# One load of the filter's rows for two blocks, in long runs, in a one-core gated mix of a state-space convolution and a spectral filter

## The chip, the cores and the metric

The kernel runs on one core of a Trainium2 chip. TensorE (PE) multiplies matrices into PSUM, VectorE (DVE), ScalarE (ACT) and GpSimd (POOL) work element by element, and SyncE (SP) issues every transfer of this kernel into one queue, in program order. The metric is the device time of one execution in microseconds (us), as the median of three runs. Lower is better.

## The reference

The input `u` has 2048 positions and 640 channels. Two results are made from it and mixed by a gate:

```python
g = _sigmoid((x * gate_w).sum(-1, keepdims=True))
# a: a long convolution of every channel with a generated kernel, plus a skip
P = jnp.exp((A * dt[:, None])[:, :, None] * pos[None, None, :])
K = 2.0 * jnp.einsum("dn,dnl->dl", C, P).real
y = jnp.fft.irfft(Uf * Kf[None, :, :], L2)[:, :, :L]
a = y + u * D_skip[None, None, :]
# b: a 2-D FFT filter over positions and channels
X = jnp.fft.rfft2(x, axes=(-2, -1)) * (w_r + 1j * w_i)
b = jnp.fft.irfft2(X, s=(S, D), axes=(-2, -1))
return g * a + (1 - g) * b
```

## The kernel before

All FFTs are products with small matrices of cosines and sines. The 640 channels are permuted and cut into four **blocks** of 160; blocks 0 and 1 are one **half**, blocks 2 and 3 the other. The work has these parts, in the order in which the code writes them down:

- `params`: the parameters of the generated kernel, in three bf16 parts each, written to DRAM (`pm_d`, `pp_d`).
- `columns`: the forward transform of `u` along the positions. `stage1` multiplies (L694) and transposes on DVE (L696), `stage2` multiplies (L711, L706), ACT copies the result out of PSUM (L756) and it is written to DRAM as `u_d` (L758).
- `responses`: the convolution kernels, from exponentials and sines on ACT (L973, L985), products on POOL and DVE (L994, L999, L1002) and matmuls (L972, L984, L1015); they go to DRAM as `k_d` (L1022).
- `gates`: the row sums for the gate.
- `spectral`: for nine groups of frequencies, the transform along the channels, the filter, and the way back (L801 to L904). `back2` multiplies (L904), ACT copies (L906), and the rows of the filtered result are written to `s3e_d`, a DRAM tensor of the form (half, 64 rows, 32 places, 320 columns), by L910 and L912. A row of 320 columns holds the 160 columns of one block and then the 160 of the other block of its half.
- `convolution`: for each block, `first` reads `k_d` (L1062) and does stage 1 of it (L694, L696). Nine calls of `unit` follow: stage 2 (L711; L706 for the odd ninth), the product with `u_d` on DVE (L1072, L1073) and POOL (L1074, L1075), and the matmuls of the way back (L1088, L1087), copied by ACT (L1090). The `u_d` that they need is read by L1145 and, for two units at a time, by L1149. Then `final` brings both results together.

`final(c, s3)` is the function in question. It first loads `te`, the filter's rows for block `c`: two transfers (L1099), one per 64 partitions, each 64 partitions x 16 places x 160 columns, that is 640 KB in runs of 640 bytes. They read what all 34 writes of that half to `s3e_d` have left, so they wait for these. Eight places of `te` at a time are multiplied by a small matrix (L1106) and scaled by the gate into `oe` on ACT (L1109). DVE transposes the convolution's result (L1113), PE multiplies it (L1121), ACT scales it into `ot` (L1126, L1127), POOL (DVE in block 3) adds `oe` (L1129), and L1131 writes the block to the output. `te`, `oe` and `ot` are one buffer each: the load for block `c` waits for the last matmul on the `te` of block `c - 1`.

The order of the instructions is not that of the code. Every operation is first noted as a unit with its inputs, outputs and a cost; a list scheduler (`order`) then picks, engine by engine, the ready unit of the highest rank. The rank is the length of the work behind the unit plus a number per function and engine, from the table `OPT["bias"]`. `OPT` also holds how far an engine looks ahead (`slack`), what a change of matmul shape on PE must gain (`hold`) and what a change of ACT's function table must (`table`). Where the scheduler foresees an idle PE, it puts in matmuls on a dead PSUM bank, which nothing reads (L265). So other numbers in `OPT` give another order of the whole program, SP's queue included, with the same work in it.

Of the kernel before, what the change touches and what calls it, by code (L numbers as in the profile page):

```python
# [151 lines left out]
    pass  # L152


OPT = {"bias": {"phases.DVE": -458537, "kgen.PE": -2536869, "unit.PE": -1194301, "mags.PE": -331203, "columns_head.SP": 260860, "columns.SP": -693714, "params.POOL": -110164, "back2.ACT": -2261149, "final.DVE": -992306, "filt.DVE": 1107470, "F": -1039852, "convolution.ACT": -592301, "front.SP": -1514751, "back2.PE": -1325765, "K": -7913, "first.SP": 1842522, "kgen.DVE": -1054315, "parts.DVE": 962846, "final.SP": 35999, "unit.ACT": 946495, "back1.POOL": 569005, "spectral.SP": -145917, "back1.DVE": 2832979, "front.DVE": -311958, "A": -375686, "params.ACT": 1555504, "front.POOL": 552518, "stage1.DVE": -353411, "convolution.SP": 251538, "unit.POOL": 1784148, "gates.DVE": -376347, "transposes.ACT": -1106844, "columns.ACT": -1333182, "back1.ACT": -83186, "parts.SP": -217602, "final.ACT": 263248, "parts.POOL": -507299, "turned.PE": -815648, "channels.ACT": -43187, "back2.SP": -726481, "params.SP": 1202525, "body.SP": -341452, "stage2.PE": 549111, "P": 705000, "final.PE": -711277, "mags.ACT": -1704667, "G": -861810, "final.POOL": 840381, "params.DVE": 151878, "kgen.ACT": -164284, "kgen.SP": -984011, "channels.DVE": 689109, "C": 828378, "stage1.PE": 535690, "product.PE": -44746, "gates.SP": -143744, "load.SP": 1167739, "phases.POOL": -21833, "unit.DVE": -288316, "transposes.PE": 469985, "turned.ACT": 852484, "turns.SP": -557358, "second_table.SP": 378902, "table.SP": 324454, "constants.SP": -319603}, "slack": {"SP": 830, "PE": 134, "POOL": 1971, "ACT": 222, "DVE": 38}, "hold": 47607, "table": 289533}


class Unit:
# [876 lines left out]
def convolution(T, A, out):  # L1035
    R, V, G, S, P, Y = T.R, T.V, T.G, T.S, T.P, T.Y
    z = Space(R, T.left)
# [56 lines left out]
    gate = lambda x, j, a: T.gate[:, x, 8 * j + a:8 * j + a + 1]  # L1094

    def final(c, s3):
        te, oe, ot = tep(), oep(), otp()
        for j in range(2):
            Y.dma_start(te[64 * j:64 * j + 64], T.s3e_d[c // 2, :, 16 * j:16 * j + 16, 160 * (c % 2):160 * (c % 2) + 160], reads=[("e", k, c // 2) for k in range(16)] + [("e1", c // 2)])  # L1099
# [15 lines left out]
        for k, (a, n) in enumerate(AS):  # L1115
            p = fin()[:, :, 0:160 * n].rearrange("p j (a d) -> p j a d", a=n)
# [20 lines left out]
    for c in range(4):  # L1137
        if c == 1:
            for pool, x in more:
                pool.bases = pool.bases + x.bases  # L1140
        side = [first(c + 1, t1[c + 1])] if c < 3 else []
        if c:
            side.append(final(c - 1, s3[c - 1]))
        ux = uxp()
        Y.dma_start(ux[:32].rearrange("p r d -> p (r d)"), T.u_d[c, :32, 16].rearrange("p r d -> p (r d)"), reads=[("u", c, 16)])  # L1145
        unit(c, t1[c], s3[c], 8, ux[:32].unsqueeze(1))
        for g in range(0, 8, 2):
            u = up()
            Y.dma_start(u, T.u_d[c, :, 0:16].rearrange("p (s g) r d -> p s g (r d)", s=2)[:, :, g:g + 2], reads=[("u", c, x) for x in (g, g + 1, g + 8, g + 9)])  # L1149
# [31 lines left out]
```

## Time and profile before

| | before |
|---|---|
| median of 3 runs | 568.64 us (567.94 to 571.13) |
| the profiled execution | 570.62 us |
| its span, first to last instruction | 568.8 us |
| mean granted clock of TensorE | 0.947 |
| PE busy | 456.8 us (80%) |
| DVE busy | 446.3 us (78%) |
| ACT busy | 327.7 us (58%) |
| POOL busy | 278.9 us (49%) |
| SP's transfers, packet time of 16 DMA engines | 47.3% |

The profiled execution took 1.8 us more than its span, and 2.0 us more than the median. All times below that stand without a unit at the left of a row are microseconds from the start of the span. In a timeline, a row gives the start, the time to the end of the last instruction in it, the engine, the line, the operation with its shape, the number of instructions (xN), and in brackets the idle time ahead of it with what ended it. An f32 matmul stands twice in the profile (x32) for each one in the program (x16). In the list of instructions of the order, xN counts the program's.

### The profile page before, as it was taken

What the parts mean: (1) busy time and instruction counts of PE and PEld (TensorE: products, weight loads), DVE (VectorE), ACT (ScalarE), POOL (GpSimd) and SP (SyncE); (2) the same over time, 40 slices, a digit from 0 to 9 for tenths busy, and PEclk for the clock granted to TensorE, in tenths of its full rate; (3) what the DMA queues carried; (4) which work ended last, traced back from release to release, by engine and by line L of the source; (5) the groups of instructions that cost most, each with busy time, mean ns of one, the idle gap of its engine ahead of it and who ended that gap; (6) DMA issues with size and microseconds to landing.
All of it is one profiled execution on the core that took longest, in us unless ns stands there. A gap on an engine that the chain in (4) does not pass through costs nothing. (4 is left out here: it accounts for less than half of the span.)

```text
span 568.8 us, 17984 instructions
## 1 busy us (share of the span) xinstructions
PE 456.8 (80%) x7712; PEld 263.6 (46%) x7712; DVE 446.3 (78%) x631; ACT 327.7 (58%) x593; POOL 278.9 (49%) x254
## 2 busy tenths in 40 slices
PE   0577769689788997998989889888988578879884
PEld 0133325345455655655555565645645234334351
DVE  7899349975499899887897978969996775787353
ACT  3131397598865986888787887222433153446553
POOL 0087006315685494674658556426243331847640
PEclk9988899899898999999999999979999897999897
DMA  8856775635711341423322234652354865384704
GB/s 260 338 187 193 264 245 178 196 122 207 237 52 52 103 136 29 140 51 106 103 78 77 57 96 116 197 156 87 94 141 148 186 115 149 119 202 120 187 2 185
DMA packets 50839, 81.22 MB, mean 143 GB/s; under 512 B 4324, under 2 KB 37288, under 8 KB 50760
## 3 DMA queue, kind: packets, MB, share of 16 engines
q1 hardware_dynamic: 50760, 80.08, 47.3%
q8 instruction: 60, 0.98, 0.7%
q14 instruction: 19, 0.16, 0.1%
HBM read 51.64 MB, written 28.43 MB: 141 GB/s over the span
## 5 line engine op out<-in xcount | busy, mean ns | idle before, releaser
L994 POOL TENSOR_TENSOR sb<-sb 128x512 f32<-128x512 f32 x80 | 111.6, 1423 | 98.7 <-ACT sb L985 89.3
L696 DVE STREAM_TRANSPOSE sb<-ps 128x1024 f32<-128x1024 f32 x40 | 80.1, 2020 | 23.3 <-PE ps L694 23.3
L984 PE MATMUL ps<-sb 52*128 52x512 bf16 x480 | 74.0, 387 | 14.4 <-DVE sb L1002 9.8
L694 PE MATMUL ps<-sb 64*128 64x512 f32 x160 | 55.1, 768 | 36.9 <-DMA sb<-in_u_l 18.3
L973 ACT ACTIVATE sb<-ps 128x512 f32<-128x512 f32 (+1 forms) x80 | 63.2, 824 | 13.1 <-PE ps L972 12.3
L1074 POOL TENSOR_TENSOR sb<-sb 128x320 f32<-128x320 f32 (+1 forms) x36 | 31.2, 866 | 77.0 <-DVE sb L1072 39.3
L711 PE MATMUL ps<-sb 64*32 64x160 f32 x2048 | 57.8, 323 | 7.5 <-DVE sb L1073 2.8
L985 ACT ACTIVATE sb<-ps 128x1024 f32<-128x1024 f32 x40 | 41.2, 1029 | 27.4 <-PE ps L984 26.7
L1090 ACT COPY sb<-ps 128x640 f32<-128x640 f32 (+1 forms) x40 | 30.0, 749 | 45.5 <-PE ps L1088 41.4
L1072 DVE TENSOR_TENSOR sb<-ps,sb 128x640 f32<-128x640 f32 (+1 forms) x36 | 28.0, 776 | 35.4 <-PE ps L711 13.0
L801 PE MATMUL ps<-sb 128*128 128x161 f32 (+4 forms) x280 | 49.5, 317 | 7.6 <-DVE sb L891 7.6
L1002 DVE TENSOR_TENSOR sb<-sb,ps 128x512 f32<-128x512 f32 x80 | 51.4, 678 | 0.0
L711 PEld LDWEIGHTS ps<-sb 64*32 64x32 f32 x2048 | 33.4, 109 | 36.8 <-issue 12.5
L756 ACT COPY sb<-ps 128x320 f32<-128x320 f32 (+1 forms) x68 | 25.6, 436 | 41.4 <-PE ps L711 25.5
L801 PEld LDWEIGHTS ps<-sb 128*128 128x128 f32 (+2 forms) x280 | 39.6, 187 | 18.7 <-issue 15.1
L999 DVE SCALAR_TENSOR_TENSOR sb<-sb,ps 128x512 f32<-128x512 f32 x40 | 27.3, 682 | 26.7 <-ACT ps L985 26.7
L985 ACT ACTIVATE ps<-ps 128x1024 f32<-128x1024 f32 x40 | 40.8, 1021 | 9.4 <-PE ps L984 6.5
L1088 PE MATMUL ps<-sb 32*64 32x160 f32 x1024 | 36.5, 326 | 12.0 <-issue 5.1
L984 PEld LDWEIGHTS <-sb 52*128 52x128 bf16 x480 | 24.2, 96 | 45.7 <-issue 34.4
L1015 PE MATMUL ps<-sb 128*32 128x64 f32 x2560 | 44.6, 222 | 0.0
L1015 PEld LDWEIGHTS ps<-sb 128*32 128x32 f32 x2560 | 38.4, 111 | 12.9 <-issue 10.1
L694 PEld LDWEIGHTS ps<-sb 64*128 64x128 f32 x160 | 15.8, 222 | 53.5 <-DVE sb L696 24.9
(128 smaller groups left out, 876.7 us busy)
## 6 DMA issues: line engine op xcount, KB each, us to landing
sb<-u_d SPq DMA_DIRECT2D x24, 640.0 KB
u_d<-sb SPq DMA_DIRECT2D x32, 320.0 KB
sb<-in_w_l SPq DMA_DIRECT2D x8, 642.0 KB
sb<-in_u_n SPq DMA_DIRECT2D x8, 640.0 KB
k_d<-sb SPq DMA_DIRECT2D x20, 256.0 KB
s3e_d<-sb SPq DMA_DIRECT2D x32, 160.0 KB
sb<-s3e_d SPq DMA_DIRECT2D x8, 640.0 KB
out<-sb SPq DMA_DIRECT2D x3, 1280.0 KB
```

The lines of the kernel that those rows point to most:

```text
L694: T.P.matmul(p[:, h].rearrange("p (d q a) -> p d q a", d=2, q=8), T.e1[l], x[l, :, i:i + 8], start=True, stop=True)
L696: T.V.transpose(t1[:, g:g + 8].rearrange("p g k d -> p g d k"), p.rearrange("p h (g d a) -> p (h g) d a", d=4, a=32))
L711: T.P.matmul(o[i][32 * j:32 * j + 32], T.w2[l, 4 * g + j, 32 * ri:32 * ri + 32], t1[l, :, 4 * g + j], start=True, stop=True)
L801: P.matmul(p[:, 161 * i:161 * i + n], lhs(i, part), tab(i)[part][0], start=i == 0, stop=False)
L973: u = S.activation(ef[:, :, c:c + n], p[:, :, :n], AF.Exp)
L984: P.matmul(p[:, h, :], st.pp[l, zz], turns[l, v, s], start=s == 0, stop=s == 2)
L985: u = S.activation(p if o is None else o, p if o is None else p.rearrange("p h (v c) -> p h v c", v=2), AF.Sin, scale=TWO_PI)
L994: G.tensor_tensor(out=y[:, v], in0=e[:, :, 64:96], in1=sc[:, 1 - v], op=ALU.mult)
L1002: V.tensor_tensor(out=xh[:, 0, h].rearrange("p d (y j) -> p d y j", y=2), in0=eh[:, h, :, 0:64].rearrange("p d (y j) -> p d y j", y=2), in ...
L1015: P.matmul(st.pb[32 * r:32 * r + 32, o, :], y[:, ri, 4 * qq + r, :], x[:, ri, 4 * qq + r, :], start=t % 2 + qq + 1 - ri == 0, stop=t % 2 + ...
L1074: G.tensor_tensor(out=t2[:nl, 0, :n], in0=ma[:nl, :n, 0], in1=ma[:nl, :n, 1], op=ALU.subtract)
L1088: P.matmul(q[o, j - js[0], 0:160], w3[l, 2 * g + s, ri, :], t2[l, ri, s, :], start=ri == 0, stop=ri == 1)
```

## The change

`te` becomes a tile of 16 places x 320 columns: the rows for both blocks of a half. It is loaded when `c` is even, by two transfers of 64 partitions x 5120 numbers (1280 KB each). In DRAM the 16 places of a row lie one behind the other, so every partition's part is one run of 20 KB. Blocks 0 and 1, and then blocks 2 and 3, take their 160 columns out of the same tile, so there are four transfers instead of eight, with the same bytes. The matmuls read the tile with a step of 320 instead of 160 from place to place. `oe` and `ot` lie 2560 numbers further on. All numbers of `OPT` are new: the order was found anew. The core of the diff:

```diff
-OPT = {"bias": {"phases.DVE": -458537, "kgen.PE": -2536869, ...}, "slack": {"SP": 830, "PE": 134, "POOL": 1971, "ACT": 222, "DVE": 38}, "hold": 47607, "table": 289533}
+OPT = {"bias": {"phases.DVE": 48428, "kgen.PE": -2202650, ...}, "slack": {"SP": 669, "PE": 73, "POOL": 354, "ACT": 7, "DVE": 65}, "hold": 54748, "table": 412949}
...
-    tep, oep, otp = z.pool(1, 16, 160), z.pool(1, 2, 8, 160), z.pool(1, 2, 8, 160)
+    tep, oep, otp = z.pool(1, 16, 320), z.pool(1, 2, 8, 160), z.pool(1, 2, 8, 160)
...
     def final(c, s3):
-        te, oe, ot = tep(), oep(), otp()
-        for j in range(2):
-            Y.dma_start(te[64 * j:64 * j + 64], T.s3e_d[c // 2, :, 16 * j:16 * j + 16, 160 * (c % 2):160 * (c % 2) + 160], reads=[("e", k, c // 2) for k in range(16)] + [("e1", c // 2)])
+        oe, ot = oep(), otp()
+        if c % 2 == 0:
+            T.te = tep()
+            for j in range(2):
+                Y.dma_start(T.te[64 * j:64 * j + 64].rearrange("p a d -> p (a d)"), T.s3e_d[c // 2, :, 16 * j:16 * j + 16].rearrange("r a d -> r (a d)"), reads=[("e", k, c // 2) for k in range(16)] + [("e1", c // 2)])
+        te = T.te[:, :, 160 * (c % 2):160 * (c % 2) + 160]
         for a, n in AS:
```

Lines behind the load stand 3 further down in the changed kernel: L1106 is now L1109, L1109 is L1112, L1121 is L1124, L1126 and L1127 are L1129 and L1130, L1129 is L1132, L1131 is L1134, L1145 is L1148, L1149 is L1152. The load itself is L1101.

The order moves at many places. Three of them are shown. The first is SP's queue around the last write of the filter's rows (L912) and the first loads of them; `u_d` and `k_d` are the inputs of the convolution's units and of stage 1 of the next block. Before:

```order
L912 DMA s3e_d<-sb 32x320 x2
L1099 DMA sb<-s3e_d 64x16x160
L1149 DMA sb<-u_d 128x2x640
L1099 DMA sb<-s3e_d 64x16x160
L1149 DMA sb<-u_d 128x2x640
L1099 DMA sb<-s3e_d 64x16x160 x2
L1062 DMA sb<-k_d 64x768 x4
L1149 DMA sb<-u_d 128x2x640
L1062 DMA sb<-k_d 64x512 x4
```

and now:

```order
L912 DMA s3e_d<-sb 32x320 x2
L1101 DMA sb<-s3e_d 64x5120 x2
L1152 DMA sb<-u_d 128x2x640 x2
L1062 DMA sb<-k_d 64x768 x4
L1152 DMA sb<-u_d 128x2x640
L1062 DMA sb<-k_d 64x512 x4
```

The `u_d` transfer that stood between the two loads of block 0 is behind both now, and the two loads of block 1, which stood ahead of `k_d`, are gone. The second place is further on in the same queue, at the loads for the second half. Before:

```order
L1131 DMA out<-sb 128x2x1280
L1149 DMA sb<-u_d 128x2x640 x2
L1099 DMA sb<-s3e_d 64x16x160 x2
L1149 DMA sb<-u_d 128x2x640 x2
L1131 DMA out<-sb 128x2x1280
L1099 DMA sb<-s3e_d 64x16x160 x2
```

and now:

```order
L1134 DMA out<-sb 128x2x1280
L1152 DMA sb<-u_d 128x2x640
L1101 DMA sb<-s3e_d 64x5120 x2
L1152 DMA sb<-u_d 128x2x640 x3
L1134 DMA out<-sb 128x2x1280 x2
```

One `u_d` transfer instead of two stands ahead of the load, three instead of two behind it.

The third place is on PE, from the last matmuls of the filter (L904) to the first ones on `te`. Before:

```order
L904 MATMUL ps<-sb 64x320 x2
L1088 MATMUL ps<-sb 64x160 x8
L711 MATMUL ps<-sb 32x160 x16
L694 MATMUL ps<-sb 128x512 x2
L1088 MATMUL ps<-sb 64x160 x8
L711 MATMUL ps<-sb 32x160 x16
L1088 MATMUL ps<-sb 64x160 x9
L1087 MATMUL ps<-sb 64x160 x2
L1088 MATMUL ps<-sb 64x160 x23
L711 MATMUL ps<-sb 32x160 x16
L694 MATMUL ps<-sb 128x512 x2
L1106 MATMUL ps<-sb 64x480 x4
```

and now, from the middle of that stretch on:

```order
L1088 MATMUL ps<-sb 64x160 x9
L1087 MATMUL ps<-sb 64x160 x2
L1088 MATMUL ps<-sb 64x160 x7
L711 MATMUL ps<-sb 32x160 x16
L1088 MATMUL ps<-sb 64x160 x16
L265 MATMUL ps<-sb 128x128 x3
L694 MATMUL ps<-sb 128x512 x2
L711 MATMUL ps<-sb 32x160 x16
L1109 MATMUL ps<-sb 64x480 x4
```

In all, 16 more of L1088, 16 more of L711 and 8 of L265 stand between L904 and the first matmul on `te` than before.

Besides, at the start of SP's queue the three transfers of stage 2's table `t_w` (352 KB each, L718), which stood ahead of the first transfers of the input `u_l`, now stand behind the first four of them.

More of the change, by code (lines that the diff above doesn't have):

```diff
@@ L152 @@
     pass
-OPT = {"bias": {"phases.DVE": -458537, "kgen.PE": -2536869, "unit.PE": -1194301, "mags.PE": -331203, "columns_head.SP": 260860, "columns.SP": -693714, "params.POOL": -110164, "back2.ACT": -2261149, "final.DVE": -992306, "filt.DVE": 1107470, "F": -1039852, "convolution.ACT": -592301, "front.SP": -1514751, "back2.PE": -1325765, "K": -7913, "first.SP": 1842522, "kgen.DVE": -1054315, "parts.DVE": 962846, "final.SP": 35999, "unit.ACT": 946495, "back1.POOL": 569005, "spectral.SP": -145917, "back1.DVE": 2832979, "front.DVE": -311958, "A": -375686, "params.ACT": 1555504, "front.POOL": 552518, "stage1.DVE": -353411, "convolution.SP": 251538, "unit.POOL": 1784148, "gates.DVE": -376347, "transposes.ACT": -1106844, "columns.ACT": -1333182, "back1.ACT": -83186, "parts.SP": -217602, "final.ACT": 263248, "parts.POOL": -507299, "turned.PE": -815648, "channels.ACT": -43187, "back2.SP": -726481, "params.SP": 1202525, "body.SP": -341452, "stage2.PE": 549111, "P": 705000, "final.PE": -711277, "mags.ACT": -1704667, "G": -861810, "final.POOL": 840381, "params.DVE": 151878, "kgen.ACT": -164284, "kgen.SP": -984011, "channels.DVE": 689109, "C": 828378, "stage1.PE": 535690, "product.PE": -44746, "gates.SP": -143744, "load.SP": 1167739, "phases.POOL": -21833, "unit.DVE": -288316, "transposes.PE": 469985, "turned.ACT": 852484, "turns.SP": -557358, "second_table.SP": 378902, "table.SP": 324454, "constants.SP": -319603}, "slack": {"SP": 830, "PE": 134, "POOL": 1971, "ACT": 222, "DVE": 38}, "hold": 47607, "table": 289533}
@@ new lines @@
+OPT = {"bias": {"phases.DVE": 48428, "kgen.PE": -2202650, "unit.PE": -166615, "mags.PE": -115174, "columns_head.SP": 872702, "columns.SP": 682166, "params.POOL": 553588, "back2.ACT": -2816928, "final.DVE": -1005244, "filt.DVE": 1993741, "F": -1335392, "convolution.ACT": -539462, "front.SP": -566676, "back2.PE": -822415, "K": -40112, "first.SP": 928307, "kgen.DVE": -160505, "parts.DVE": 1478799, "final.SP": 305754, "unit.ACT": 847620, "back1.POOL": 1387462, "spectral.SP": -399574, "back1.DVE": 2754302, "front.DVE": -1043326, "A": -2049249, "params.ACT": 2087046, "front.POOL": 669673, "stage1.DVE": -1769657, "convolution.SP": 201784, "unit.POOL": 3697225, "gates.DVE": -149497, "transposes.ACT": -2172258, "columns.ACT": 49354, "back1.ACT": -371473, "parts.SP": -1042272, "final.ACT": 647227, "parts.POOL": -1006977, "turned.PE": -1910767, "channels.ACT": 43010, "back2.SP": -770465, "params.SP": 1391786, "body.SP": 596739, "stage2.PE": 1093838, "P": 1629575, "final.PE": -357097, "mags.ACT": -1663446, "G": -1187815, "final.POOL": 395975, "params.DVE": -671244, "kgen.ACT": -1412550, "kgen.SP": -887462, "channels.DVE": -303793, "C": 857506, "stage1.PE": -187598, "product.PE": -671984, "gates.SP": -488191, "load.SP": 1427459, "phases.POOL": -154283, "unit.DVE": -213280, "transposes.PE": -438092, "turned.ACT": 2426795, "turns.SP": -766223, "second_table.SP": 550791, "table.SP": 900949, "constants.SP": 335628}, "slack": {"SP": 669, "PE": 73, "POOL": 354, "ACT": 7, "DVE": 65}, "hold": 54748, "table": 412949}
```

## The prediction

> **What bounds the kernel now.** I read the page first, then the table of 50 us stretches, then the timelines of the stretch in which PE is least busy, and last the transfers that run there.
>
> ```profile
> core 0: us, PE busy (x) PEld busy (x) DVE busy (x) ACT busy (x) POOL busy (x), PEclk, DMA share, GB/s
> 200.00:250.00 50.00, 43.86 (x728) 27.34 (x727) 45.33 (x72) 39.18 (x63) 33.66 (x30) 1.00 0.32 93
> 450.00:500.00 50.00, 37.80 (x648) 16.75 (x650) 33.31 (x35) 20.05 (x52) 20.45 (x21) 0.86 0.55 138
> ```
>
> In the middle of the kernel PE and DVE share the work and both are almost full: 43.86 and 45.33 us of 50. From 450 us on, in the convolution, PE has 12.2 us of 50 idle and DVE 16.7, at a granted clock of 0.86. What ends this idle time?
>
> ```profile
> 447.50 1.01 PE L1106 MATMUL ps<-sb 64*64 64x480 f32 x2
> 453.62 1.87 PE L1106 MATMUL ps<-sb 64*64 64x480 f32 x6 [5.11 <-DMA sb<-s3e_d]
> 455.43 1.32 PE L711 MATMUL ps<-sb 64*32 64x160 f32 x32
> 459.39 0.89 PE L711 MATMUL ps<-sb 64*32 64x160 f32 x32
> ...
> 463.58 0.80 PE L1088 MATMUL ps<-sb 32*64 32x160 f32 x32 [0.28 <-ACT sb L1090]
> 464.32 1.13 PE L694 MATMUL ps<-sb 64*128 64x512 f32 x4
> 465.49 0.52 PE L1088 MATMUL ps<-sb 32*64 32x160 f32 x12
> 471.12 1.33 PE L1088 MATMUL ps<-sb 32*64 32x160 f32 x20 [5.11 <-issue]
> 472.38 1.32 PE L711 MATMUL ps<-sb 64*32 64x160 f32 x32
> 473.63 1.37 PE L1088 MATMUL ps<-sb 32*64 32x160 f32 x32
> 474.93 2.08 PE L694 MATMUL ps<-sb 64*128 64x512 f32 x4
> ```
>
> Two stalls of 5.11 us each. The first waits for the rows of the filter (`s3e_d`), in the middle of the first matmuls on `te`. The second has no releaser in the profile. Behind the first, DVE runs dry too (and behind the second, whose L711 comes late):
>
> ```profile
> 456.91 0.83 DVE L1072 TENSOR_TENSOR sb<-ps,sb 128x640 f32<-128x640 f32 x1 [5.61 <-issue]
> ```
>
> So time won in these two places is time won at the end, as long as nothing else is late there. After each stall the same matmuls run slower for some us (L711 1.32 us instead of 0.89), so a stall costs more than its idle time. Now the transfers, first SP's issues, then the data rate from 440 to 454 us in 40 steps of 0.35 us:
>
> ```profile
> 440.08 0.60 SPq L1099 DMA_DIRECT2D sb<-s3e_d  x1
> ...
> 441.73 0.60 SPq L1099 DMA_DIRECT2D sb<-s3e_d  x1
> ...
> 459.50 1.30 SPq L1099 DMA_DIRECT2D sb<-s3e_d  x2
> ```
>
> ```profile
> GB/s 84 0 0 0 88 59 163 338 294 183 174 174 172 190 188 201 146 190 358 388 386 333 174 168 192 187 176 177 176 179 181 266 190 219 368 360 309 103 29 22
> DMA packets 2645, 2.65 MB, mean 190 GB/s; under 512 B 78, under 2 KB 2136, under 8 KB 2643
> ```
>
> The 640-byte runs of `te` move at 168 to 201 GB/s; `u_d` between and behind them, in runs of 2560 bytes, at 333 to 388. One load of 0.66 MB therefore takes about 3.7 us, and the second half of `te` arrives only at 453 us, 13 us after the first issue.
>
> **The change, part by part.** The sum is made against the profiled execution (570.6 us) and then carried to the median, which is 2.0 us lower.
>
> *Stall 1.* How fast are runs of 20 KB? No row has any. The nearest are a load of the filter's weights in runs of 5136 bytes, alone (172 to 176 us, steps of 0.1 us), and an output write in runs of 5120 bytes, alone (555 to 560 us, steps of 0.125 us):
>
> ```profile
> GB/s 0 0 0 0 0 0 0 0 0 0 51 257 0 154 257 0 257 154 103 103 360 205 411 308 514 360 565 257 565 257 616 154 514 103 52 0 0 0 0 0
> DMA packets 144, 0.66 MB, mean 164 GB/s; under 512 B 16, under 2 KB 16, under 8 KB 144
> ```
>
> ```profile
> GB/s 0 0 0 0 0 0 0 0 0 532 410 369 451 369 451 410 287 573 369 369 492 246 532 328 369 532 328 451 410 328 532 410 287 614 41 0 0 0 0 0
> DMA packets 272, 1.31 MB, mean 262 GB/s; under 512 B 16, under 2 KB 16, under 8 KB 272
> ```
>
> 0.66 MB in 25 steps is 264 GB/s, 1.31 MB in 25 steps is 420. The new pair, 2.62 MB, so takes 6.2 to 9.9 us instead of the 14 us that its bytes take at 190. From the first issue (440.08) to the first of its bytes pass about 1.4 us, and from the last bytes (about 452.7) to PE's restart 0.9: the new tile is there at 448.6 to 452.4, if the last write of the filter stays where it is. PE came for it at 447.50; the new order puts 16 of L1088 (0.80), 16 of L711 (0.89) and 8 of L265 (about 2.1) ahead, so it comes between 449.2 (the L265 in idle time) and 451.3. What is left of the wait is 0 to 3.2 us; I take 0, since the middle of both ranges is at 450.4. Saved: 5.11, and the slow matmuls behind (1.32 - 0.89 for L711, and 1.87 for six of L1106 where eight take 1.04, row below, so 1.1): together **-6.6 us** (bounds -6.6 and -1.9). The other loads of `te` ended no wait on PE, so their halving is worth nothing by itself.
>
> ```profile
> 492.05 1.04 PE L1106 MATMUL ps<-sb 64*64 64x480 f32 x8
> ```
>
> The Trainium skill speaks against this term: its page "DMA: Bandwidth & Descriptors", section Specifications, puts the smallest transfer for line rate at 512 B, so 640-byte runs would lose nothing and 20 KB would gain nothing. The rates above, 168 to 201 against 333 to 388 GB/s in the same 14 us, don't agree with it. It is a rival below.
>
> *Stall 2.* PE stops in the middle of a block of matmuls whose data is there. What is late are its instructions, I think:
>
> ```profile
> q8 instruction: 60, 0.98, 0.7%
> ...
> 460.90:468.10 7.20, 4.78 (x116) 2.17 (x112) 6.60 (x6) 2.48 (x5) 3.40 (x4) 1.00 1.09 191
> ...
> q8 instruction: 1, 0.02, 8.4%
> ```
>
> The 60 packets on the instruction queue match PE's 15,424 instructions at 257 each. One of them runs at 468 to 469 us (the last row, of that 1 us), and PE goes on at 471.12. From 461 to 468 the 16 DMA engines were full (share 1.09), with the pair of `te` that was issued at 459.50 in front and the `k_d` and `u_d` of the next units behind. That pair is gone from this place. The stall's price is 5.11 and the slow matmuls behind it, 1.33 - 0.50, 1.32 - 0.89, 1.37 - 0.80 and 2.08 - 1.13, in sum 2.8: **7.9 us**. Whether the packet of this moment meets other transfers in the new order can't be read from here (`k_d` and `u_d` still run), so I take half, **-4.0** (bounds -7.9 and 0).
>
> The same can hit the new pairs, which fill the DMA engines for 6.2 to 9.9 us.
>
> ```profile
> 436.00:440.00 4.00, 3.68 (x86) 1.95 (x72) 1.83 (x3) 1.62 (x3) 2.92 (x5) 1.00 0.11 28
> ```
>
> PE runs 158 instructions in 4 us here, so 257 last 6.5 us. A packet that has to wait for a whole pair comes up to 3.4 us late, and its own time (8.4% of 16 engines in 1 us: 1.3 us) and the restart (up to 3 us) come on top: 0 to 6.6, middle 3.3. Two pairs at one half each: **+3.3** (0 to 13).
>
> The Trainium skill ("Runtime: NRT & Kernel Launch", Instruction fetch mechanics) holds the fetch of the next 256 instructions to be mostly hidden. By it both of these terms fall out, and the result is 0.7 us higher; the gap between 465.49 and 471.12 has then no cause that I can name.
>
> *SP's queue.* Eight issues of `te` become four; at about 0.6 us each that is 2.4 us on an engine that waits most of the time: 0. The `u_d` transfer that is now behind the pair lands at 449 to 454 (the pair's end and 0.66 MB at 360 GB/s) instead of 448; it belongs to the last two units of block 1, and their L711 come after the matmuls on `te` in both orders: 0.
>
> *The start.* `t_w` (1.08 MB) is behind the first input now.
>
> ```profile
> 20.38 2.00 DVE L696 STREAM_TRANSPOSE sb<-ps 128x1024 f32<-128x1024 f32 x1 [2.06 <-PE ps L694]
> ```
>
> PE can start 3 to 4 us sooner (1.08 MB at the 260 and 338 GB/s of the first two slices), but DVE is the fuller engine and has 2.06 us idle to give. Bounds -2.1 and 0 (work that moves up here can wait later); I take 0.
>
> *The rest of the order.* The same instructions stand in another order from the second us on. After L904 DVE has the same 27 L1072, 26 L1073 and 10 L696 to do, PE 16 of L711 and of L1088 more, which then lie no longer ahead of it: 0. For the middle there is only a bound: DVE idles 4.7 us of 50 in the row above, so some 33 in the 350 us from 100 to 450, and an eighth more or less of that is +-4 us.
>
> Sum: -6.6 - 4.0 + 3.3 = -7.3. From 570.6 that is 563.3; from the median of 568.6 it is **561.3 us**.
>
> **The rivals.**
>
> *The stall moves to the second half (slower).* In the new queue the second pair has one `u_d` transfer ahead of it whose buffer DVE must free, and three behind.
>
> ```profile
> SPq L1149 <- DVE sb L1073: 52.1, 10, 10.1
> 510.75 1.84 PE L1121 MATMUL ps<-sb 128*64 128x480 f32 x8
> ...
> 515.93 3.29 PE L1121 MATMUL ps<-sb 128*64 128x320 f32 x8
> ```
>
> From the last matmul on block 1's rows to the first on block 2's, the new order has 64 of L1088 (3.2), 48 of L711 (2.7), 4 of L694 (2.3) and L1121's successor (1.84 and 3.29): 13.3 us of PE. The pair needs 1.4 + 6.2 to 9.9 + 0.9 = 8.5 to 12.2, so it is in time unless SP is held for more than 1 to 5 us when that last matmul ends. Held as long as before's longest such wait, 10.1 us, PE would stand for up to 9.0 us, and then run slowly as above, for 1.5 to 2.8: 561.3 + 11.2 = 572.5. Against it: before, SP waited for PE at this load and not the other way round. Chance 0.13.
>
> *Long runs are no faster per byte.* The pair then takes 14 us, arrives at 440.1 + 1.4 + 13.8 + 0.9 = 456.2, and PE waits 4.9 to 7 us as before, once; stall 2 is as in the forecast: 561.3 + 6 = 567.3, about the same as before. The page named at stall 1 would have it so. For it: 64 partitions only, in two transfers, as before. Against it: both rows with long runs are over 260 GB/s. Chance 0.10.
>
> *The gain is given back.* The tile comes in time, but the new order loses 4 us in the middle and a packet of instructions is late once more: 561.3 + 5 = 566.3. Chance 0.12.
>
> *Both stalls go and none comes.* 568.6 - 6.6 - 7.9 and half of the start's 2.1 = 553 us. For it: from 440 to 540 us the DMA engines have less to do: 5.24 MB of `te` at 264 to 420 instead of 190 GB/s is 8 to 15 us less. Chance 0.12.
>
> **How the numbers follow.** The forecast has the remaining 0.53, with its own range of 556 to 565. A measurement of this kernel can tell 0.5% (2.8 us) from no change. Faster than 565.8: the forecast's 0.53, all of the last rival, 0.04 of the middle two: 0.69. Within: 0.17. Slower than 571.5: 0.13 of the first rival and 0.01 of the others. The range takes in the last rival's upper half and reaches to the middle of the slower cases: 554.5 to 570.
>
> **What would show it.** Right: no wait of L1109 for `s3e_d`; the pair moves at over 260 GB/s; no PE stall without a releaser between the first pair and the next block; the stretch from L904 to the end, 131.5 us now (437.27 to 568.8), is shorter by 5 to 12 us. Wrong: PE waits for `s3e_d` at the first or the third block's L1109 (the row with its idle time names it), the pair moves at under 200 GB/s, or L904 comes several us later than 437.27.
>
> ```profile
> 437.27 0.76 PE L904 MATMUL ps<-sb 64*64 64x320 f32 x4 [0.32 <-POOL sb L894]
> ```

## The result, and the profile after

The changed kernel takes **591.07 us** (median; 584.75 to 598.15), and the kernel before, run beside it, 569.68 us. The ratio is 1.035 (95% interval 1.029 to 1.042): 3.5% slower, where the prediction said 561.3 us and gave "slower" 0.14. The ratios here and below leave disturbed runs out, so they are not exactly the quotient of the medians beside them. The profiled execution took 591.9 us (span 589.9).

The prediction named L904 as a signpost: before, its last run began at 437.27. In the timeline of PE after the change:

```profile
452.83 0.76 PE L904 MATMUL ps<-sb 64*64 64x320 f32 x4
...
468.24 0.59 PE L265 MATMUL ps<-sb 128*128 128x128 f32 x2 [2.90 <-issue]
472.01 1.86 PE L1109 MATMUL ps<-sb 64*64 64x480 f32 x2
475.75 1.87 PE L1109 MATMUL ps<-sb 64*64 64x480 f32 x6 [1.89 <-DMA sb<-s3e_d]
```

L904 is 15.6 us late, and the new load has not run yet: it reads what L904 makes. So three quarters of the loss (21 us) lie ahead of the thing that was changed, and the rest behind: from this L904 to the end it is 137.1 us (589.9 - 452.83), where it was 131.5. One profile's L904 is only good to some microseconds, though: in four more profiles of before's order, from the runs below, it lies between 432.5 and 441.9, and in two more of the new order, with nothing changed in the middle, at 452.7 and 454.3. Behind L904, PE still waits for `s3e_d` (1.89 us here, 1.03 at the third block), and its instructions are still late (2.90 us, "issue").

What happens ahead of L904? The table of stretches, first of the kernel before, then of the changed one (columns: stretch, its length, busy time of PE, of PE's weight loads, DVE, ACT and POOL with instructions, granted clock, DMA share, GB/s):

```profile
230.00:368.00 138.00, 123.33 (x2104) 79.58 (x2101) 121.49 (x199) 107.40 (x170) 83.93 (x73) 1.00 0.33 98
368.00:437.00 69.00, 60.23 (x805) 38.00 (x803) 59.30 (x86) 21.82 (x51) 27.56 (x31) 0.95 0.47 137
```

```profile
230.00:368.00 138.00, 122.05 (x2054) 79.89 (x2050) 107.16 (x181) 106.31 (x167) 81.13 (x71) 0.91 0.28 80
368.00:437.00 69.00, 59.00 (x725) 38.34 (x726) 60.92 (x87) 19.82 (x44) 23.48 (x26) 0.90 0.46 131
```

In the same 138 us PE is as busy as before, but at a clock of 0.91 where it had 1.00, and DVE does 14 us less work. PE is idle only 1.3 us longer; it is slower. The rows of PE's timeline that have a wait of 1 us or more between 220 and 350 us say where this begins. Before:

```profile
223.42 0.79 PE L801 MATMUL ps<-sb 128*128 128x161 f32 x4 [1.38 <-DVE sb L891]
256.62 0.79 PE L801 MATMUL ps<-sb 128*128 128x161 f32 x4 [1.33 <-DVE sb L891]
290.08 0.79 PE L801 MATMUL ps<-sb 128*128 128x161 f32 x4 [1.38 <-DVE sb L891]
323.27 0.79 PE L801 MATMUL ps<-sb 128*128 128x161 f32 x4 [1.33 <-DVE sb L891]
```

And after, with the two runs of L1015 around the third wait:

```profile
226.35 0.79 PE L801 MATMUL ps<-sb 128*128 128x161 f32 x4 [3.09 <-DVE sb L891]
260.01 0.28 PE L972 MATMUL ps<-sb 50*128 50x256 bf16 x1 [2.85 <-DVE sb L1002]
...
293.32 1.10 PE L1015 MATMUL ps<-sb 128*32 128x64 f32 x64
297.26 0.39 PE L972 MATMUL ps<-sb 50*128 50x256 bf16 x1 [2.84 <-DVE sb L1002]
...
298.58 1.93 PE L1015 MATMUL ps<-sb 128*32 128x64 f32 x64
...
333.85 0.28 PE L972 MATMUL ps<-sb 50*128 50x256 bf16 x1 [2.85 <-DVE sb L1002]
```

Once per spectral group there is one such wait, in both kernels. Before, it is L801 that waits for L891, for 1.4 us. After, the first is the same wait, grown to 3.09 us, and the other three are another one, of L972 for L1002, at 2.85 us. Behind the third, the same 64 matmuls of L1015 take 1.93 us, where they took 1.10 at 293.32, just ahead of it: half the clock. Within 2.4 us of the end of each of these four gaps the records of the clock begin to show half speed, for 3.4, 6.8, 10.2 and 6.8 us (in steps of 3.41 us), 27 us in all; before, there is none between 200 and 370 us.

DVE's timeline shows where the wait for L1002 comes from, here the third. Before:

```profile
283.88 0.82 DVE L870 TENSOR_TENSOR sb<-sb 128x642 f32<-128x642 f32 x1
284.61 0.68 DVE L1002 TENSOR_TENSOR sb<-sb,ps 128x512 f32<-128x512 f32 x1
285.21 0.96 DVE L871 TENSOR_TENSOR sb<-sb 128x321 f32<-128x321 f32 x1
```

After:

```profile
291.56 0.81 DVE L870 TENSOR_TENSOR sb<-sb 128x642 f32<-128x642 f32 x1
292.29 1.23 DVE L1021 TENSOR_TENSOR sb<-sb 128x8 f32<-128x8 f32 x1
293.44 0.48 DVE L871 TENSOR_TENSOR sb<-sb 128x321 f32<-128x321 f32 x1
293.85 1.56 DVE L872 TENSOR_TENSOR sb<-sb 128x321 f32<-128x321 f32 x1
295.33 0.68 DVE L999 SCALAR_TENSOR_TENSOR sb<-sb,ps 128x512 f32<-128x512 f32 x1
295.93 0.68 DVE L1000 TENSOR_TENSOR sb<-sb,ps 128x512 f32<-128x512 f32 x1
296.52 1.27 DVE L1002 TENSOR_TENSOR sb<-sb,ps 128x512 f32<-128x512 f32 x2
```

L999, L1000 and L1002 are the last readers of a PSUM bank (`pair`) into which PE's next L972 writes. Before, only the last L1002 of this set was left when L870 ended. In the new order L1021, L871 and L872 stand ahead of all of them. None of this has to do with `te`; it came in with the table of numbers that sets the order.

### The profile page after: what moved, and what is told of

It is laid out like the page before. It is cut to its first block, busy times and chain, and to the rows that moved or that the text cites. A ratio compares the mean times of both kernels' runs of the same rounds, so it can differ in the third digit from the quotient of the medians.

```text
span 589.9 us, 18056 instructions
## 1 busy us (share of the span) xinstructions
PE 476.6 (81%) x7736; PEld 276.8 (47%) x7736; DVE 441.6 (75%) x631; ACT 327.3 (55%) x593; POOL 275.0 (47%) x254
## 5 line engine op out<-in xcount | busy, mean ns | idle before, releaser
L994 POOL TENSOR_TENSOR sb<-sb 128x512 f32<-128x512 f32 x80 | 107.8, 1370 | 105.4 <-ACT sb L985 95.0
L694 PE MATMUL ps<-sb 64*128 64x512 f32 x160 | 55.9, 774 | 37.3 <-DVE sb L696 19.4
L984 PE MATMUL ps<-sb 52*128 52x512 bf16 x480 | 71.8, 388 | 13.0 <-DVE sb L1002 6.4
L973 ACT ACTIVATE sb<-ps 128x1024 f32<-128x1024 f32 (+1 forms) x80 | 62.1, 822 | 20.4 <-PE ps L972 19.8
L1074 POOL TENSOR_TENSOR sb<-sb 128x320 f32<-128x320 f32 (+1 forms) x36 | 30.0, 835 | 84.0 <-PE ps L1088 47.0
L711 PE MATMUL ps<-sb 64*32 64x160 f32 x2048 | 58.6, 327 | 11.9 <-ACT sb L756 5.8
L801 PE MATMUL ps<-sb 128*128 128x161 f32 (+4 forms) x280 | 53.5, 340 | 3.1 <-DVE sb L891 3.1
L711 PEld LDWEIGHTS ps<-sb 64*32 64x32 f32 x2048 | 33.8, 110 | 44.0 <-DVE sb L1073 14.4
L1002 DVE TENSOR_TENSOR sb<-sb,ps 128x512 f32<-128x512 f32 x80 | 51.3, 680 | 0.0
L801 PEld LDWEIGHTS ps<-sb 128*128 128x128 f32 (+2 forms) x280 | 44.0, 206 | 14.9 <-issue 13.1
L999 DVE SCALAR_TENSOR_TENSOR sb<-sb,ps 128x512 f32<-128x512 f32 x40 | 27.4, 684 | 30.0 <-ACT ps L985 27.9
L1015 PE MATMUL ps<-sb 128*32 128x64 f32 x2560 | 46.8, 228 | 0.9 <-ACT sb L1020 0.8
L1015 PEld LDWEIGHTS ps<-sb 128*32 128x32 f32 x2560 | 40.5, 115 | 14.4 <-issue 12.0
L838 PE MATMUL ps<-sb 128*128 128x128 f32 (+1 forms) x216 | 35.3, 302 | 8.5 <-DVE sb L862 1.9
L694 PEld LDWEIGHTS ps<-sb 64*128 64x128 f32 x160 | 15.9, 225 | 54.8 <-DVE sb L696 27.6
```

The source lines that it names most:

```text
L694: T.P.matmul(p[:, h].rearrange("p (d q a) -> p d q a", d=2, q=8), T.e1[l], x[l, :, i:i + 8], start=True, stop=True)
L711: T.P.matmul(o[i][32 * j:32 * j + 32], T.w2[l, 4 * g + j, 32 * ri:32 * ri + 32], t1[l, :, 4 * g + j], start=True, stop=True)
L801: P.matmul(p[:, 161 * i:161 * i + n], lhs(i, part), tab(i)[part][0], start=i == 0, stop=False)
L838: P.transpose(o, src[:nl, x, e0:e1], T.id[:nl, :nl])
L973: u = S.activation(ef[:, :, c:c + n], p[:, :, :n], AF.Exp)
L984: P.matmul(p[:, h, :], st.pp[l, zz], turns[l, v, s], start=s == 0, stop=s == 2)
```

## The experiments

In all runs below the order is written out as a list, one entry per piece of work, instead of being found anew; so one thing can be changed while every engine's sequence stays. "Before's order" and "the new order" are the two lists. The lists themselves, of some 2230 entries, are left out of the code below, and so are other parts, marked by `...`.

### Load alone, order alone

First the two halves of the change, each by itself: before's list with the new pair of loads, and the new list with the old eight loads.

```diff
-        R.emit(order(R.units, OPT))
+        R.emit(frozen(R.units))
```

> The order of before, unit by unit as a fixed list, with the new load: the two transfers of 1280 KB stand where block 0's and block 2's two stood, block 1's and block 3's are taken out. Nothing else moves. Theory 'order' (the loss is made by the new order of the parts ahead of the convolution, where 15 of the 21 us already stand at the last L904, before the load has run once): within 1% of before, 564 to 573 us. The first wait on the filter's rows should even be longer than the 5.1 us of before: both transfers were seen at about 200 GB/s in the changed kernel, so 2.62 MB are there at 441.5 + 13 + 0.9 = 455.4, 8 us after PE came for them; against it stands that block 1's load is gone from 459.5, and with it perhaps the second stall (8 us). Theory 'load' (the longer transfers themselves hold up the rest): 580 us or more.

Measured: 570.86 us, ratio 1.003 (0.999 to 1.007).

> The order of the changed kernel as a fixed list, with the loads of before: block 0's and block 2's two transfers stand where the long ones stood, those of block 1 and 3 go in right behind the last matmul that reads the tile before. Theory 'order': the slow middle stays, 586 to 598 us. Theory 'load': 575 us or less.

Measured: 586.07 us, ratio 1.026 (1.018 to 1.034), with the same waits of 2.83 to 3.09 us in the middle. So the order carries the loss, and the new load gains nothing even where the order is the old one. Why nothing? PE's timeline of the new load in before's order, at the place of the two stalls:

```profile
449.51 1.45 PE L1109 MATMUL ps<-sb 64*64 64x480 f32 x2 [2.47 <-DMA sb<-s3e_d]
458.53 1.87 PE L1109 MATMUL ps<-sb 64*64 64x480 f32 x6 [7.57 <-DMA sb<-s3e_d]
...
465.90 1.41 PE L694 MATMUL ps<-sb 64*128 64x512 f32 x4 [0.30 <-ACT sb L1112]
467.24 0.88 PE L1088 MATMUL ps<-sb 32*64 32x160 f32 x32
468.05 0.88 PE L711 MATMUL ps<-sb 64*32 64x160 f32 x32
```

The first stall has grown from 5.11 us to 2.47 + 7.57 = 10.04. The second (5.11 us, no releaser) is gone. Plus 5 and minus 5 cancel, and so do the times, within the interval. The 128 packets of the pair run from 440.8 to 457.5 and, for the second half, from 504.6 to 519.3: 2.62 MB in 16.7 and 14.7 us is 157 and 178 GB/s (218 and 222 with the other transfers of these stretches), no more than the old 640-byte runs (168 to 201).

### Which rate has a load into 64 partitions?

A load of the same 2.62 MB in one transfer over all 128 partitions, in before's order; the rows then land in the wrong partitions, so the filter's part of the output is mixed up, and only the time counts.

```diff
-            for j in range(2):
-                Y.dma_start(T.te[64 * j:64 * j + 64]..., T.s3e_d[c // 2, :, 16 * j:16 * j + 16]...)
+            Y.dma_start(T.te.rearrange("p a d -> p (a d)"), T.s3e_d[c // 2].rearrange("r (j a) d -> (r j) (a d)", j=2), ...)
```

> As the fixed order of before with the new load, but each half is loaded by one transfer over all 128 partitions (20 KB runs as before). The rows land in other partitions than the matmuls want, so the filter's part of the output is mixed up; the work is the same in number and size. Theory 'partitions' (a transfer into 64 partitions gets half the rate, whatever its runs): 2.62 MB at about 400 GB/s are there at 441.5 + 6.6 + 0.9 = 449, so the first wait falls to 1 to 2 us and the kernel is 5 to 9 us faster than with the same order and two transfers: 557 to 566 us. Theory 'runs' (20 KB runs are slow as such, about 12.7 GB/s on each DMA engine): no difference to two transfers.

Measured: 555.88 us, ratio 0.977 (0.969 to 0.985): faster, as the theory of the partitions had it. The runs are 20 KB in both. What differs is the number of partitions in one transfer and, with it, that there is one transfer and not two.

Then the rate by itself: a kernel without computation, which loads one tile at a time.

```diff
+              y.dma_start(t[0:64, 0:5120], u[0:64, 0:5120])
+              y.dma_start(t[:, 0:2560], u[:, 0:2560])
+              y.dma_start(t[0:64, 0:2560].rearrange("p (a d) -> p a d", d=160), v[0:64, 0:16, 0])
+              y.dma_start(t[:, 0:1280].rearrange("p (a d) -> p a d", d=160), v[:, 0:8, 0])
+              y.dma_start(t[0:64, 0:5120].rearrange("p (a d) -> p a d", d=640), ...)
+              y.dma_start(t[:, 0:5120], u[:, 0:5120])
+              y.dma_start(t[0:32, 0:10240], u[0:32, 0:10240])
```

> Leaves the whole computation out and writes zeros: seven loads from the input u_n, each waiting until the one before has landed, twice: 64 partitions x 20 KB; 128 x 10 KB; 64 partitions x 16 runs of 640 bytes; 128 x 8 runs of 640 bytes; 64 x 8 runs of 2560 bytes; 128 x 20 KB; 32 x 40 KB. Then four writes of 1280 KB. Theory 'partitions': 64 partitions at about 200 GB/s for all three run lengths, 128 at 350 to 420, 32 at about 100. Theory 'runs': 640 bytes at 170 to 200 for both partition counts, 2560 bytes at 350, 20 KB the same for 64 and 128.

The stretches from the first to the last packet of each load, in this sequence (the last column is GB/s; all loads were repeated, with rates within 4%; the first, the third and the last stretch miss a few packets at their ends: by the packets they are 192, 186 and 190 GB/s):

```profile
2.10:8.90 6.80, 1.42 (x1) 0.00 (x0) 1.00 0.84 178
10.60:14.90 4.30, 0.00 (x0) 0.00 (x0) 1.00 0.88 305
16.90:20.50 3.60, 0.00 (x0) 0.00 (x0) 1.00 0.87 182
22.50:25.20 2.70, 0.00 (x0) 0.00 (x0) 1.00 0.84 243
27.10:34.00 6.90, 0.00 (x0) 0.00 (x0) 1.00 0.90 189
35.90:43.20 7.30, 0.00 (x0) 0.00 (x0) 1.00 0.92 359
44.80:51.70 6.90, 0.00 (x0) 0.00 (x0) 1.00 0.77 166
```

The lower 64 partitions in runs of 20 KB, 640 bytes and 2560 bytes: 192, 186 and 189 GB/s. There the run's length changes next to nothing. All 128 partitions: 305 in runs of 10 KB, 243 in runs of 640 bytes, 359 in runs of 20 KB. So the lower 64 have about half the rate of all 128 in runs of 20 KB, and three quarters in runs of 640 bytes. But the rate does not follow the number of partitions: 32 in runs of 40 KB are as fast as 64 (6.9 us for the same 1.31 MB), where the theory had half of it.

Is it their number, or which ones they are? A second kernel of loads alone (parts (c) to (f) of it):

```diff
+              y.dma_start(t[0:128:2, 0:5120], u[0:128:2, 0:5120])
+              y.dma_start(t[32:96, 0:5120], u[32:96, 0:5120])
+              y.dma_start(t[0:96, 0:5120], u[0:96, 0:5120])
+              y.dma_start(t[0:128, 0:5120], u[0:128, 0:5120])
```

> No computation: the output is written as zeros, and only the loads before it matter, each alone, runs of 20 KB per partition, twice over. (a) partitions 0 to 63, then 64 to 127, on SP's queue one behind the other; (b) the same two at once, the second on ACT's queue; (c) the 64 even partitions; (d) partitions 32 to 95; (e) partitions 0 to 95; (f) all 128. Theory 'count' (a load of 64 partitions runs at half rate whichever they are): a 13.6 us, b 7.3 if the queues add up, c and d 6.8 each, f 7.3. Theory 'which' (the rate goes by the half of the partitions that is reached; 0 to 63 have one half of the ports): a 13.6, b 7.3 to 13, c and d half of that, 3.7 each (355 GB/s), e about 6.8 (its 64 lower partitions bound it), f 7.3. The Trainium skill ("SBUF - State Buffer", Door 1: The DMA port swizzle) has the second, with 196 GB/s for partitions 0..63 and 328 for all 128 at 1 MiB, and only +6% for two loads on the two halves at once, which would make b about 12.8.

Stretches of (c) to (f), first to last packet:

```profile
29.70:33.90 4.20, 0.00 (x0) 0.00 (x0) 1.00 0.84 312
35.90:40.00 4.10, 0.00 (x0) 0.00 (x0) 1.00 0.84 310
41.60:50.80 9.20, 0.00 (x0) 0.00 (x0) 1.00 0.92 211
52.60:60.10 7.50, 0.00 (x0) 0.00 (x0) 1.00 0.90 347
```

It is which ones. The 64 even partitions, and the 64 from 32 to 95, have 310 GB/s, while the 64 lower ones, the first load of (a), take 6.7 us for their 1.31 MB, which is 195. Both loads of (a), the lower and then the upper 64 on one queue like the changed kernel's pair, take 12.9 us for 2.62 MB, 203 GB/s, though together they fill all 128 partitions. The load of 96 took 9.2 us; that its 64 lower partitions hold it back would give 6.8, so this is not explained. Part (b), two queues at once, told nothing: the second load had to wait until (a) had been read, and began when the first was nearly over.

The Trainium skill has this rule ("SBUF — State Buffer", Door 1: The DMA port swizzle): SBUF has 16 ports for transfers, partitions 0 to 63 reach only 8 of them, and 0..31 are as fast as 0..63; it gives 196 GB/s for 0..63 and 328 for all at 1 MiB. The runs agree: 192, and 305 to 359.

### A single load whose rows are in their places

Before's order again, one transfer over 128 partitions, but with the source read as two blocks of 64 rows, so that every row is where the matmuls look for it.

```diff
+            Y.dma_start(T.te.rearrange("p a d -> p (a d)"), T.s3e_d[c // 2].rearrange("r (j a) d -> j r (a d)", j=2), ...)
```

> The kernel before's order on every engine, with the pair of loads of a half replaced by one load whose destination is all 128 partitions (2.62 MB, runs of 20 KB; its source is read as two blocks of 64 rows, so that every row lands in the partition where the matmuls look for it). Computes the reference. Partitions theory (64 partitions are served at about 190 GB/s whatever the runs, 128 at about 355, as the isolated loads show): the load takes 7 to 8 us instead of 13 to 14, PE waits 2 to 3 us for it once, and the median is 553 to 559, as with the load that mixes up the rows (555.9). Rival (the fast result came from the mixed-up rows, which read DRAM in one piece of 2.62 MB; here the source is 128 pieces of 20 KB in another sequence): 566 to 572.

Measured: 641.07 us, ratio 1.132 (1.125 to 1.138). Both theories missed. PE's timeline and the data rate from 438 to 492 us in 40 steps:

```profile
491.50 1.88 PE L1109 MATMUL ps<-sb 64*64 64x480 f32 x8 [46.61 <-DMA sb<-s3e_d]
```

```profile
GB/s 32 135 349 47 73 46 61 101 292 148 36 61 61 46 46 61 61 61 46 46 61 61 46 46 61 61 61 46 46 61 61 46 46 61 61 61 46 46 51 46
```

Some 50 GB/s: each packet is as fast as in the fast load (0.76 us for 20 KB), but only two are under way at a time instead of 13 to 14. The outermost step of the source has size 2 here. The Trainium skill ("DMA: Bandwidth & Descriptors", Why a DMA increments its semaphore by 16 and not by 1) says so of loads from the queues of SP and ACT: the number of DMA engines is the largest, up to 16, that divides the outermost size of both sides. Two packets at a time agree with it.

So the source needs 128 equal steps, which is a matter of how `s3e_d` is laid out. For that its columns are written in another sequence (the table of constants is permuted), in two writes per row block where there was one.

```diff
-        T.s3e_d = dram.tile([2, 64, 32, 320], F32, name="s3e_d")
+        T.s3e_d = dram.tile([2, 2, 64, 16, 320], F32, name="s3e_d")
...
-                Y.dma_start(T.s3e_d[hf, 4 * kk:4 * kk + 4].rearrange("(e r) a d -> (r a) e d", e=2), s3[l], ...)
+                for e in range(2): Y.dma_start(T.s3e_d[hf, :, 4 * kk + 2 * e:4 * kk + 2 * e + 2].rearrange("j r a d -> (r a) j d"), s3[l, e], ...)
...
+            Y.dma_start(T.te.rearrange("p a d -> p (a d)"), T.s3e_d[c // 2].rearrange("j r a d -> (j r) (a d)"), ...)
```

> The kernel before's order, with s3e_d laid out as (half, j, row, 16, 320), so that one load of 2.62 MB with 128 equal steps fills all 128 partitions of te; the columns of the table of constants t_w3 are permuted for it, and each write of s3e_d (L910) becomes two of 80 KB. Computes the reference. Partitions theory: the load spreads over all 16 DMA engines (the slow one, whose source had j as its outermost step of 2, used two of them) and takes 7 to 8.5 us as with the mixed-up rows (555.9), less what 32 more issues on SP cost (0.4 us each on a queue that mostly waits): 553 to 560. Rival (the additional writes of 1280-byte runs delay the last rows of s3e_d, or SP's other loads): 562 to 570.

Measured: **560.3 us, ratio 0.983 (0.976 to 0.989)**: 1.7% faster than the kernel before, the best version of this study that computes everything, 0.3 us above the theory's 553 to 560 and below the rival's 562 to 570. The load runs from 446.1 to 454.4 (8.3 us) and from 498.9 to 506.0 (7.1 us). PE's timeline at its first use:

```profile
441.90 0.76 PE L904 MATMUL ps<-sb 64*64 64x320 f32 x4 [0.29 <-POOL sb L894]
...
454.74 1.04 PE L1109 MATMUL ps<-sb 64*64 64x480 f32 x8 [2.54 <-DMA sb<-s3e_d]
```

One wait of 2.54 us is left of the two stalls of 5.11. The end lies 117.8 us behind this L904 (559.7 - 441.9), where it was 131.5. That is 13.7 us less, but in this profile L904 itself comes 4.6 us later than before. Whether the additional writes of `s3e_d` do that is not shown; with the load of mixed-up rows, without these writes, L904 comes at 432.53.

### Is the order's loss the clock?

The new order as it is, with nine dummy matmuls (L265, on a PSUM bank that nobody needs then) ahead of the four matmuls at which PE stands once per group. The waits themselves stay. An entry of the list is the number of a piece of work, the dummy matmuls ahead of it, and their bank:

```diff
-... (1211, 0, 1) ... (753, 0, 1) ... (848, 0, 1) ... (939, 0, 1) ...
+... (1211, 9, 1) ... (753, 9, 1) ... (848, 9, 1) ... (939, 9, 1) ...
```

> The changed kernel with its own order on every engine; on PE nine dummy matmuls of L265 (about 0.23 us each) are put ahead of the four matmuls at which PE stands for 2.84 to 3.09 us once per spectral group (226.35, 260.01, 297.26 and 333.85 us). What these matmuls wait for, DVE's L891 and L1002, is untouched, so the gaps end when they did; PE is only kept busy in them. Theory A (the order's loss is multiplied by the clock: a gap of about 3 us is followed by 3.4 to 10.3 us at half clock, 27 us in all after these four, in which PE does half its work): these stretches go back to full clock, and of their price of up to 27/2 = 13.6 us some 5 to 12 come back, since DVE hides a part; the last L904 comes at 441 to 448 instead of 452.8 and the median is 579 to 586. Theory B (the late DVE instructions are the loss and the clock only goes with it): 589 to 593, and L904 stays within 2 us of 452.8.

Measured: 579.99 us, ratio 1.024 (1.016 to 1.033), against 1.035 for the changed kernel. The intervals still touch, so the profile has to decide. The timeline of PE at the third gap, and the stretches:

```profile
291.69 1.10 PE L1015 MATMUL ps<-sb 128*32 128x64 f32 x64
292.72 2.27 PE L265 MATMUL ps<-sb 128*128 128x128 f32 x18
295.64 0.28 PE L972 MATMUL ps<-sb 50*128 50x256 bf16 x1 [0.65 <-DVE sb L1002]
...
296.64 1.10 PE L1015 MATMUL ps<-sb 128*32 128x64 f32 x64
```

```profile
230.00:368.00 138.00, 124.29 (x2133) 82.35 (x2132) 117.24 (x197) 107.31 (x170) 82.45 (x72) 0.99 0.32 90
368.00:437.00 69.00, 60.81 (x758) 39.52 (x758) 60.63 (x87) 20.49 (x47) 23.70 (x26) 0.87 0.39 112
```

PE still waits for L1002, but behind it L1015 takes 1.10 us. The clock of the first stretch is back from 0.91 to 0.99, and DVE does 10 us more in it, though nothing was changed on DVE. L904 comes at 446.78 instead of 452.83. Time, clock and L904 are as theory A had them. In the second stretch the clock is still low, 0.87.

The other way is to shorten these gaps, by making DVE's instructions come sooner at three of the four places. The order of the lines on DVE there:

```diff
-  L871, L872, L999, L1000, L1002, L1002, L873
+  L999, L1000, L1002, L1002, L871, L872, L873
```

> The changed kernel with one move on DVE at three places (the gaps at 260, 297 and 334 us): L871 and L872 of the filter (0.48 and 1.56 us) go behind the L999, L1000, L1002, L1002 for whose PSUM bank PE's L972 waits, so that these come 2.0 us sooner. Nothing else moves. Theory A (clock): the three gaps fall from 2.85 to about 0.8 us, no half clock follows them (24 us in all before), and 3 x 2.0 us of the gap and some of the 12 us of the half clock come back: median 576 to 584, L904 at 438 to 446. Theory B (gap alone): at most 3 x 2.0 = 6 us, 585 to 589. Theory C (DVE is the bound there and PE's gaps cost nothing): 589 to 593.

Measured: 583.41 us, ratio 1.028 (1.021 to 1.036), at the slow end of theory A (576 to 584) and just below B (585 to 589); the interval reaches into both. L904 comes at 448.17, later than A's 438 to 446. The timeline says why the gain is small:

```profile
294.62 0.28 PE L972 MATMUL ps<-sb 50*128 50x256 bf16 x1 [0.95 <-DVE sb L1002]
...
298.55 0.66 PE L838 MATMUL ps<-sb 128*128 128x128 f32 x4 [1.61 <-DVE sb L891]
```

The gap falls from 2.84 to 0.95 us, but a new one of 1.61 comes 4 us later. By itself this run does not tell A from B.

Then dummy matmuls at four more gaps of the run with the first four filled: 4 ahead of L694 at 362.74, 6 ahead of L694 at 378.66, 4 ahead of L711 at 401.23 and 6 ahead of L711 at 429.79.

> The changed kernel as in the run with the four gaps filled (580.0), with dummy matmuls of L265 at four more gaps of PE: 4 before the L694 at 362.74 (1.44 us, waits for k_d), 6 before the L694 at 378.66 (2.06, L696), 4 before the L711 at 401.23 (1.41, L1073), 6 before the L711 at 429.79 (1.94, L1073). Theory (clock): the half clock that remains between 365 and 441 (3.4 + 3.4 + 6.8 + 10.2 = 23.8 us in steps of 3.4) goes for the most part, and of its price of up to 12 us some 4 to 9 come back: 571 to 576, L904's last start at 438 to 443. Rival (those stretches have other causes, such as PE waiting in many small pieces, or DVE is the bound there): 578 to 582.

Measured: 574.33 us, ratio 1.009 (1.004 to 1.013). Stretches and L904:

```profile
230.00:368.00 138.00, 125.39 (x2095) 82.91 (x2085) 114.93 (x193) 105.35 (x166) 82.59 (x72) 0.99 0.32 91
368.00:437.00 69.00, 63.33 (x850) 42.08 (x846) 64.19 (x91) 23.74 (x55) 25.83 (x28) 1.00 0.45 129
```

```profile
438.09 0.76 PE L904 MATMUL ps<-sb 64*64 64x320 f32 x4
```

56 dummy matmuls, and no other instruction moved, take the ratio from 1.035 to 1.009, with intervals far apart. L904 is back to 438.1 (437.3 before). So the theory of the clock holds for most of the 15.6 us. One reservation: before has a gap of 3.22 us at 372 and a clock of 0.95 in the second stretch, so a part of what the last four fillings gain would have been there to gain before, too. In two other profiles of before's order (the load of mixed-up rows, and the one at 50 GB/s) no half clock followed that gap, the second stretch had 1.00, and L904 came at 432.53 and 434.61. Against these, with the clock kept up in both, the new order is 3.5 to 5.6 us late, which the 0.9% of time that is left fits.

### Do load and order add?

The single load over 128 partitions in the new order, without and with the filled gaps:

> The changed kernel's order with the same layout and the same single load over 128 partitions. In the changed kernel PE waits 2.9 us in two places for te, and the packets of instructions come 2.9 and 0.8 us late behind the pair. Theory (those go with a load of 7 to 8 us, and the half clock behind them): 581 to 587, against 591 of the changed kernel. Rival (the loss before L904 hides the load; the waits move elsewhere): 588 to 592.

Measured: 580.59 us, ratio 1.023 (1.017 to 1.030): 1.2% less than the changed kernel. There PE waits 0.39 us for `s3e_d`, and 0.42 us without a releaser where it was 2.90.

> Both together: the changed kernel's order with all eight gaps filled and with the single load over 128 partitions. Whether the parts add: theory (clock and load are separate losses): the result of the filled gaps less 4 to 10 us, 562 to 571. Rival (the load's gain is hidden once the front is faster): within 2 us of the filled gaps alone.

Measured: 565.89 us, ratio 0.997 (0.994 to 1.001): 1.15% less than with the filled gaps alone. Within the intervals, of 0.4 to 0.7% to each side, the load is worth the same with a slow front as with a fast one, so the two parts are separate and add.

## Why the prediction was wrong, point by point

**What bounds the kernel** was read rightly: the stalls were on the path. The load over 128 partitions, which shortens them, made the kernel 1.7% faster in before's order.

**Stall 1 (-6.6) failed**, at the step "0.66 MB in 25 steps is 264 GB/s, 1.31 MB in 25 steps is 420. The new pair so takes 6.2 to 9.9 us". Both rows were of transfers over all 128 partitions, and one of them was a write; the pair is two transfers of 64. It took 14.7 and 13.5 us in the changed kernel, 16.7 in before's order, and the wait there grew to 10.04 us: +4.9 instead of -5.1. In the changed kernel the wait came out at 1.89 us, inside the bounds of 0 to 3.2, but that is luck: PE stood 2.90 us for its instructions just ahead and so came later, and the two together are 4.79 us where 5.11 had been. The row that the prediction had for 64 partitions, `te` at 168 to 201 GB/s, was laid to its short runs. The rival "long runs are no faster per byte" named the right reason ("64 partitions only, in two transfers, as before") and got 0.10. There is a second effect that the step passed over: half of the new tile is needed at first, but all of it has to be there. The old loads brought the first block's half alone.

**Stall 2 (-4.0)** was right in its mechanism and too small. In before's order, with the pair gone from 459.50, the stall is gone whole (-5.1 of idle time alone), which fits a packet of instructions that had to wait behind that pair. The DMA records of the traces bear it out: PE goes on 1.4 to 1.6 us behind the end of a 16 KB packet on the instruction queue, before (469.50 and 471.12), in the changed kernel (466.81 and 468.24) and with the old loads in the new order (467.74 and 469.15). **The same hazard at the new pairs (+3.3)** was right in size: 2.90 and 0.81 us of "issue" in the changed kernel, beside the pairs; with the faster load 0.42 us is left of the first and nothing of the second. It is not the long runs' doing, though: with the old loads in the new order there are 2.38 us at the same place, and with the new pair in before's order none over 0.2.

**SP's queue (0) and the start (0)** hold: at 179 us, where L878 of the first filter group ends on DVE, the changed kernel is 0.7 us behind, and from 450 us on neither PE nor DVE waits for `u_d`.

**The rest of the order (0, +-4 from an eighth of DVE's idle time) failed, and it alone turned the sign**: 15.6 us before L904. The bound was built from the wrong engine and took a longer wait to cost what it lasts. DVE's idle time says how much work could be shifted; the price came from PE, where the longest wait of each group grew by 1.5 us and each time half a clock followed for 3.4 to 10 us. The prediction had one piece in hand, that matmuls behind a stall run slower (1.32 us instead of 0.89), and used it for two stalls only. The other, the new order of DVE in which L871 and L872 stand ahead of L999, it did not look at.

**The rivals.** The stall in the second half came as 1.03 + 0.81 us, not 9. "The new order loses 4 us in the middle" was the nearest, and had a quarter of the size. None of them reached 591.

**What would show it**: L904 late by several us was named as a sign of "wrong", and so was a pair under 200 GB/s; both came. The stretch from L904 to the end, which should have become 5 to 12 us shorter, became 5.5 us longer.

What stays open: when a gap costs half a clock. Length alone does not decide. Gaps of 2.83 to 3.10 us were followed by it 13 times out of 13, but the 3.2 us of before's order in three of five profiles only; 1.33 to 1.38 us were harmless four times out of four in the kernel before, but behind 1.40 us at 407.54 in the changed kernel half a clock lasted 6.8 us. In each trace the records of the clock all begin on one grid of 3.41 us, and how busy PE was within a step of this grid sorts the cases better. Over all twelve kernels that compute, between 100 and 540 us, a step at full clock was followed by one at half clock in 24 of 24 cases when PE was busy for less than 40% of it, in 28 of 32 at 40 to 50%, in 25 of 46 at 50 to 60%, in 13 of 205 at 60 to 80%, and in 3 of 1070 above. So where a gap falls in the grid should matter, but no run moves a gap within it. The remaining 0.9% of the new order with all gaps filled was not taken apart.

## What to carry to other kernels

Before sizing a transfer, look at which partitions it fills and what its outermost step is: here the 64 lower partitions had 192 GB/s where all 128 had 359, and an outermost step of 2 cut it to a seventh. When an order is found anew, compare the recurring waits of PE in the steady part before anything else: here the longest one grew from 1.4 to 2.9 us, once in 35 us, and filling four such gaps, with the waits left as they were, gave back 6.05 us at L904, about as much again as the waits had grown. A few dummy matmuls in such a gap tell in one run whether the clock is the reason.

## What the runs showed of the hardware

- A load into partitions 0 to 63 ran at 186 to 196 GB/s with runs of 640 bytes to 20 KB; 64 partitions from both halves (the even ones, or 32 to 95) at 302 to 317 with runs of 20 KB; all 128 at 305 to 359 with runs of 10 and 20 KB. A load of the lower 64 and one of the upper 64, one behind the other on one queue, had 203 together.
- A load whose source has an outermost size of 2 had two packets under way at a time and ran at 50 GB/s.
- Half clock came in steps of 3.41 us on one grid, after steps in which PE was busy for less than about half (52 of 56 steps under 50%); nine dummy matmuls (18 rows of L265, 2.27 us) in gaps of 2.84 to 3.09 us kept it away, four times out of four. The Trainium skill ("TensorE: Matmul & The Clock Gate", HAM oscillation — how this bites in real kernels) asks for no idle gap over about 3.4 us. The step of 3.41 us agrees with its window; the limit does not: 2.84 us were too long here.
